# The second mixture ahead of the loop, as straight-line code

## The chip, the cores and the metric

One core of a Trainium2 chip runs the kernel. The metric is device time in microseconds, the median of three runs.

## The reference

Three layers follow each other on 4 batches of 576 tokens and 512 columns. The first two (a landmark attention and a gated feed-forward layer) end ahead of the change. The third, the mixture, is this:

```python
skip_score = x @ w_skip
do_compute = skip_score > 0
out = x.copy()
xc = x[do_compute]
logits = xc @ w_gate
e_idx = np.argmax(logits, axis=1)
...                                   # gate_w: softmax weight of the chosen expert
for e in range(E):                    # E = 8
    mask = e_idx == e
    if not mask.any():
        continue
    h = np.maximum(xc[mask] @ w1[e], 0.0)
    y[mask] = gate_w[mask, None] * (h @ w2[e])
out[do_compute] = xc + y
```

A token has one expert at most, w1 of an expert is 512 x 1024, w2 is 1024 x 512.

## The kernel before

The rows of x are handled in eight units of 288 tokens, two per batch. Each unit ends with a `finish` that writes x to `out` and the weight of each token for each expert to a table `m_d`, and sums these weights per batch and expert into `Ms`. The mixture works on pairs (expert e, batch b): a pair takes all 576 rows of a batch through one expert, and multiplies the result by the column of `m_d`, which is zero for tokens of other experts. Pairs whose sum in `Ms` is zero are left out, by a list made on the chip.

`list_pairs` (line 985) makes such a list: it flags the pairs with a sum over zero (`fl`), counts the flags ahead of each with a product by a triangular matrix, and by further small products puts the experts, the batches and the number of listed pairs into one row of integers, `lst`. It is called twice: in `early`, before the last unit, for the first pair, and in `others`, beside the first mixture, for the rest ("rest", without that first pair). `pair_at` (line 1025) reads entry i of a list into registers of SP, which alone uses them, as addresses of DMAs. `number` (line 1022) reads the length into registers of all engines, for the loop.

`mixture` (line 1101) does one pair, in straight order: for eight blocks f of 128 hidden columns it splits a block of w2 into a high and a low part (ScalarE, then GpSimd or VectorE), makes two accumulators `ph` (288 tokens each, 12 matmuls each: high by high, high by low, low by high, over four row blocks), and takes them out through ScalarE (the relu, high part) and VectorE (the remainder, low part). At f = 5 `load_rows` (line 1071) issues on SP the loads of the column of `m_d` (`mc`) and of the five blocks of `out` (`old`). After f = 7 it asks `nxt` for the next pair and issues that pair's loads on SP: x (`load_x`), w1 (`load_w1`), which are split at once, and w2 (`load_w2`), which stay raw until the next pair's blocks f. Then come the w2 products: five output blocks `py` (16 and four times 24 matmuls), each followed by a VectorE operation `old = py * mc + old` and a write of `old` to `out`. With `ahead` False a mixture loads its own w2 first; only the first mixture does.

The first mixture is straight-line code (lines 1350 to 1352). Behind it stands the loop over the list "rest" (lines 1354 to 1356), whose body is one mixture:

```python
npairs = number(rest[0])
with tc.For_i(0, npairs) as i:
    e, b = pair_at(rest[0], i)
    drain(mixture(e, b, lambda: pair_at(rest[0], i + 1), True))
```

All DMAs are issued by SP. Within a stretch of straight code, and within the loop's body, the compiler orders each engine's queue by its own plan, so a queue can differ from the order of the code. The accumulators `acc` are four banks, `pb` two (`bank`). `Paced` (line 36) books an estimate for every call of an engine into `busy`; in the last unit `slot` uses these sums to decide where side work goes.

Of the kernel before, what the change touches and what calls it, by code (L numbers as in the profile page):

```python
# [6 lines left out]
F32 = mybir.dt.float32  # L7
F32R = mybir.dt.float32r
I32 = mybir.dt.int32
ALU = mybir.AluOpType  # L10
# [20 lines left out]
LP = 40  # L31
# [31 lines left out]
def attention_moe_kernel(  # L63
# [4 lines left out]
    V, A, G, PE = (  # L68
        Paced(e, busy, n)
        for e, n in (  # L70
            (nc.vector, "V"), (nc.scalar, "A"), (nc.gpsimd, "G"), (nc.tensor, "P")
        )
    )
# [3 lines left out]
    def pool(stack, name, bufs=1, **kw):  # L77
        return stack.enter_context(tc.tile_pool(name=name, bufs=bufs, **kw))
# [31 lines left out]
    rt = pool(ph1, "rt")  # L110
# [7 lines left out]
    start, start1 = ExitStack(), ExitStack()  # L118
# [23 lines left out]
    def bank(name):  # L142
        return pb.tile([128, 512], F32, name=name, tag="b")
# [12 lines left out]
    ones = const.tile([128, 32], F32, name="ones")  # L156
# [828 lines left out]
    def list_pairs(name, but=None):  # L985

        pq = bank("pq")
        PE.matmul(
            pq[0:32, 0:1], Ms.rearrange("p b e -> p (b e)"), ones[:, 0:1],
            start=True, stop=True,  # L990
        )
        fl = rt.tile([32, 1], F32, name="fl")
        if but is None:
            V.tensor_scalar(fl, pq[0:32, 0:1], 0.0, None, ALU.is_gt)
        else:
            V.scalar_tensor_tensor(
                fl, pq[0:32, 0:1], 0.0, but, ALU.is_gt, ALU.subtract
            )
        pq = bank("pq")
        PE.matmul(pq[0:32, 0:1], tri, fl, start=True, stop=True)  # L1000
        ps = rt.tile([32, 1], F32, name="slot")
        V.tensor_copy(ps, pq[0:32, 0:1])
        oh = const.tile([32, LP], F32, name=f"oh{name}")
        V.tensor_scalar(oh, pos, ps, fl, ALU.is_equal, ALU.mult)
        pl = bank("pl")
        PE.matmul(pl[0:1, 0:LP], pair[:, 1:2], oh, start=True, stop=True)
        PE.matmul(pl[0:1, LP : 2 * LP], pair[:, 2:3], oh, start=True, stop=True)
        PE.matmul(
            pl[0:1, 2 * LP : 2 * LP + 1], fl, ones[0:32, 0:1], start=True, stop=True
        )  # L1010
        lst = const.tile([1, 2 * LP + 1], I32, name=name)
        V.tensor_copy(lst, pl[0:1, 0 : 2 * LP + 1])
        return lst, oh[:, 0:1]

    SPE = mybir.EngineType.SP

    def ld(lst, idx, mx):
        return nc.values_load(
            lst[0:1, bass.ds(idx, 1)], engines=(SPE,), min_val=0, max_val=mx
        )  # L1020

    def number(lst):
        return nc.values_load(lst[0:1, 2 * LP : 2 * LP + 1], min_val=0, max_val=B * E)

    def pair_at(lst, i):
        return ld(lst, i, E - 1), ld(lst, i + LP, B - 1)
# [29 lines left out]
    def w2raw(f):  # L1056

        return w2r_t[f // 2][:, f % 2]
# [7 lines left out]
    def load_x(b, c, eng):  # L1066
        r = late.tile([128, S], F32, name="x2r", tag="ld", bufs=4)
        SP.dma_start(r, xT_d[:, c, bass.ds(b * S, S)])
        rsplit(eng, xs[0][:, c], xs[1][:, c], r)

    def load_rows(e, b):

        mc = late.tile([128, 5], F32, name="mc")
        mrow = m_d[bass.ds(b * S, S), bass.ds(e, 1)]
        with nc.allow_non_contiguous_dma(reason="one column"):
            SP.dma_start(
                mc[:, 0:4], mrow[0:512].rearrange("(t p) o -> p (t o)", p=128)
            )
            SP.dma_start(mc[0:64, 4:5], mrow[512:576])
        orow = out[bass.ds(b * S, S), :]  # L1080
        olds = []
        for t in range(5):
            m = 128 if t < 4 else 64
            old = late.tile([128, DM], F32, name=f"old{t}")
            SP.dma_start(old[0:m], orow[128 * t : 128 * t + m, :])
            olds.append(old)
        return mc, orow, olds

    def early(res):

        lst, res["mark"] = list_pairs("lst")
        e, b = res["pair"] = pair_at(lst, 0)
        for c in range(KC):
            load_x(b, c, V if c % 2 else G)
        yield
        for i in range(2):
            for f in range(4 * i, 4 * i + 4):
                load_w1(e, f, V if f % 2 else G)
            yield

    def mixture(e, b, nxt, ahead):

        hs = []
        for f in range(FC2):
            if ahead:
                r = w2raw(f)
            else:
                r = late.tile([128, S], F32, name="w2r", tag="ld", bufs=4)[:, 0:DM]
                load_w2(e, f, r)
            rsplit(V if f % 2 else G, *w2s(f), r)  # L1110
            wh, wl = (t.rearrange("p (c f) -> p c f", c=KC) for t in w1s(f))

            hh, hx, hl = (
                hroom[f][:, s] for s in (slice(0, S), slice(512, 640), slice(640, None))
            )
            for t in range(2):
                ts = slice(NH * t, NH * t + NH)
                ps = accbank("ph")[:, 0:NH]
                for c in range(KC):
                    xh, xl = xs[0][:, c, ts], xs[1][:, c, ts]  # L1120
                    PE.matmul(ps, wh[:, c], xh, start=(c == 0), stop=False)
                    PE.matmul(ps, wh[:, c], xl, start=False, stop=False)
                    PE.matmul(ps, wl[:, c], xh, start=False, stop=(c == KC - 1))
                A.activation(hh[:, ts], ps, AF.Relu)
                n = (NH, 512 - NH)[t]
                V.scalar_tensor_tensor(
                    hl[:, NH * t : NH * t + n], ps[:, 0:n], 0.0,
                    hh[:, NH * t : NH * t + n].bitcast(F32), ALU.max, ALU.subtract,
                )
            V.scalar_tensor_tensor(  # L1130
                hx[:, 64:128], ps[:, n:NH], 0.0, hx[:, 0:64].bitcast(F32),
                ALU.max, ALU.subtract,
            )
            hs.append((hh, hx, hl))
            if f == FC2 - 3:
                mc, orow, olds = load_rows(e, b)
            yield
        en, bn = nxt()
        if not w2r_t:
            w2r_t.extend(wo_tile(F32) for _ in range(FC2 // 2))  # L1140
        for c in range(KC):
            load_x(bn, c, V)
        for f in range(FC2):
            load_w1(en, f, V if f % 2 else G)
        for f in range(FC2):
            load_w2(en, f, w2raw(f))

        ps = accbank("py")
        for f in range(FC2):
            for i, w in enumerate(w2s(f)):  # L1150
                PE.matmul(
                    ps, hs[f][1], w,
                    start=(f + i == 0), stop=(f + i == FC2),
                )
        old = olds[4][0:64]
        for p in (ps[0:64], ps[64:128]):
            V.scalar_tensor_tensor(old, p, mc[0:64, 4:5], old, ALU.mult, ALU.add)
        SP.dma_start(orow[512:S, :], old)
        yield
        for t in range(4):  # L1160
            ts = slice(128 * t, 128 * t + 128)
            old = olds[t]
            ps = accbank("py")
            for f in range(FC2):
                (hh, _, hl), (wh, wl) = hs[f], w2s(f)
                PE.matmul(ps, hh[:, ts], wh, start=(f == 0), stop=False)
                PE.matmul(ps, hh[:, ts], wl, start=False, stop=False)
                PE.matmul(ps, hl[:, ts], wh, start=False, stop=(f == FC2 - 1))
            V.scalar_tensor_tensor(
                old, ps, mc[:, t : t + 1], old, ALU.mult, ALU.add  # L1170
            )
            SP.dma_start(orow[ts, :], old)
            yield
# [14 lines left out]
    def drain(g):  # L1188
        for _ in g:
            pass  # L1190
        if g in side:
            side.remove(g)
# [103 lines left out]
    for u in range(1, 2 * B):  # L1296
        b, half = u // 2, u % 2
# [25 lines left out]
        if u == 2 * B - 2:  # L1323
# [5 lines left out]
            first = {}  # L1329
# [3 lines left out]
    rest = []  # L1333

    def others():
        yield from fin[0]
        rest.append(list_pairs("rest", first["mark"])[0])
        yield

    oth = others()  # L1340
# [2 lines left out]
    for g in side[:]:  # L1343
        drain(g)

    def after_first():
        drain(oth)
        return pair_at(rest[0], 0)

    for _ in mixture(*first["pair"], after_first, False):  # L1350
        next(oth, None)
        next(oth, None)
    npairs = number(rest[0])
    with tc.For_i(0, npairs) as i:  # L1354
        e, b = pair_at(rest[0], i)
        drain(mixture(e, b, lambda: pair_at(rest[0], i + 1), True))
    ph1.close()
    ctx.close()

# [32 lines left out]
```

## Time and profile before

| | us |
|---|---|
| runs: 726.9, 723.27, 725.94; median | 725.94 |
| the profiled execution | 730.47 |
| its span, first to last instruction | 728.7 |
| TensorE busy | 667.1 (92%) |
| VectorE busy | 459.2 (63%) |
| ScalarE busy | 295.1 (41%) |
| GpSimd busy | 145.1 (20%) |
| mean granted clock of TensorE | 0.952 of full speed |

Times in the rows are microseconds from the start of the span, unless they are means in ns. PE is TensorE's matmul, PEld its weight load, DVE VectorE, ACT ScalarE, POOL GpSimd, SP SyncE; a q behind a name is the engine's instruction queue. L12 is a line of the kernel; as all engine calls pass through the helper `call`, they have its line, L58, and are told apart by their tiles: `ph` are the w1 products of the mixtures, `py` their w2 products. Ends of matmuls are modelled. In the profiled execution the first mixture's `ph` begin at 557.9 us, and the two trips of the loop begin with `ph` at 613.57 and 669.83 us.

### The profile page before, as it was taken

The page shows a single profiled execution, that of the slowest core. Times are in us where ns is not written, and L with a number is a line of the kernel's source. Part 1 is how long each engine was busy: PE and PEld are TensorE (multiplying, and loading weights), DVE is VectorE, ACT ScalarE, POOL GpSimd, SP SyncE. Part 2 cuts the span into 40 slices and gives each one's busy share as a digit, 9 for nine tenths or more (in the row PEclk, how much of TensorE's full clock was granted, in tenths as well). Part 3 has the DMA queues.
Part 4 walks back from the last instruction along what each step waited for, and adds up shares of the span by engine and source line. Part 5 has one row for each costly group of instructions (what it writes and reads, how often), then busy time and mean ns, then how long its engine had stood idle before and what let it go on. Part 6 is the DMA issues. An engine that isn't in the chain of part 4 may idle for free. (4 is left out here: it accounts for less than half of the span.)

```text
span 728.7 us, 13382 instructions
## 1 busy us (share of the span) xinstructions
PE 667.1 (92%) x4961; PEld 573.5 (79%) x4961; DVE 459.2 (63%) x1016; ACT 295.1 (41%) x641; POOL 145.1 (20%) x162
## 2 busy tenths in 40 slices
PE   5468799789999899999999999999999999997997
PEld 5257367678877599977898897899889988986985
DVE  5984888978887577886467966261553463352451
ACT  0773887753314431433341344240443243241340
POOL 4000024313200140220040130040362023021120
PEclk8765799899999999999999999999999999998999
DMA  8686464573125842226732107230541375462344
GB/s 284 216 248 227 143 217 152 176 180 100 46 86 117 196 128 75 93 67 149 187 84 66 64 20 157 69 75 1 166 139 62 101 218 173 130 201 95 128 140 156
DMA packets 79435, 97.12 MB, mean 133 GB/s; under 512 B 16016, under 2 KB 58000, under 8 KB 79376
## 3 DMA queue, kind: packets, MB, share of 16 engines
q1 hardware_dynamic: 79376, 96.33, 44.9%
q8 instruction: 37, 0.61, 0.4%
q14 instruction: 22, 0.18, 0.1%
HBM read 76.97 MB, written 19.34 MB: 132 GB/s over the span
## 5 line engine op out<-in xcount | busy, mean ns | idle before, releaser
L58 PE MATMUL o<-h_t,wo 128*128 128x288 f32 x1152 | 169.6, 303 | 9.2 <-ACT wo L58 3.8
L58 PEld LDWEIGHTS o<-h_t,wo 128*128 128x128 f32 x1152 | 157.9, 191 | 19.2 <-issue 6.7
L58 POOL TENSOR_TENSOR h_t<-h,h_t 128x288 fp32r<-128x288 f32 x96 | 82.2, 860 | 399.9 <-ACT h_t L58 363.8
L58 PE MATMUL pg<-ap_t,P 128*128 128x288 f32 x576 | 104.1, 306 | 3.6 <-DVE h L58 1.8
L58 PE MATMUL pv<-ap_t,P 128*128 128x288 f32 x576 | 98.8, 301 | 2.7 <-DVE h L58 2.4
L58 PEld LDWEIGHTS pg<-ap_t,P 128*128 128x128 f32 x576 | 83.2, 189 | 17.6 <-issue 10.3
L58 PEld LDWEIGHTS pv<-ap_t,P 128*128 128x128 f32 x576 | 82.8, 189 | 8.8 <-DVE h L58 4.1
L58 PE MATMUL ph<-xsh,P 128*128 128x288 f32 x384 | 80.5, 303 | 4.5 <-PEq L1354 4.5
L58 PEld LDWEIGHTS ph<-xsh,P 128*128 128x128 f32 x384 | 64.0, 194 | 5.4 <-issue 5.4
L58 DVE SCALAR_TENSOR_TENSOR h<-h,pg 128x288 f32<-128x288 f32 x96 | 42.5, 447 | 26.3 <-ACT h L58 25.2
L58 PE MATMUL ph<-xsl,P 128*128 128x288 f32 x192 | 57.9, 302 | 0.0
L58 ACT ACTIVATE h<-pg 128x288 f32<-128x288 f32 x96 | 38.9, 410 | 42.4 <-PE pg L58 39.1
L58 ACT CAST h_t<-h 128x288 fp32r<-128x288 f32 x96 | 40.8, 430 | 32.6 <-DVE h L58 32.0
L58 PE MATMUL py<-wo,h_t 128*128 128x512 f32 x210 | 51.6, 395 | 0.3 <-DVE h_t L58 0.3
L58 PEld LDWEIGHTS py<-wo,h_t 128*128 128x128 f32 x210 | 39.3, 188 | 10.2 <-issue 0.8
L58 DVE TENSOR_TENSOR h<-h,pv 128x288 f32<-128x288 f32 x96 | 42.4, 446 | 5.9 <-PE pv L58 3.0
L58 DVE STREAM_TRANSPOSE T<-kq 64x576 f32<-64x576 f32 (+1 forms) x40 | 35.6, 889 | 9.0 <-DMA kq<-in_q_dram 4.6
L58 DVE TENSOR_TENSOR P<-P,P 128x512 fp32r<-128x512 f32 x48 | 31.7, 685 | 12.5 <-ACT P L58 12.1
L58 ACT CAST P<-P 128x512 fp32r<-128x512 f32 x48 | 26.3, 588 | 31.8 <-PE P L58 31.6
L58 PEld LDWEIGHTS ph<-xsl,P 128*128 128x128 f32 x192 | 37.4, 195 | 0.1
L58 POOL TENSOR_TENSOR P<-w1r,P 128x512 fp32r<-128x512 f32 x16 | 21.4, 1341 | 66.3 <-ACT P L58 66.3
L58 DVE SCALAR_TENSOR_TENSOR old<-py,mc,old 128x512 f32<-128x512 f32 (+1 forms) x18 | 13.5, 749 | 31.4 <-PE py L58 31.2
(230 smaller groups left out, 967.2 us busy)
## 6 DMA issues: line engine op xcount, KB each, us to landing
wl<-wg_d SPq DMA_DIRECT2D x36, 256.0 KB, 4.7
wr<-wv_d SPq DMA_DIRECT2D x32, 256.0 KB, 4.8
w1r<-in_moe_w_dram SPq DMA_DIRECT2D x32, 256.0 KB, 3.2
wr<-in_moe_w_gate_dram SPq DMA_DIRECT2D x6, 1024.0 KB, 6.6
wr<-in_moe_w_val_dram SPq DMA_DIRECT2D x6, 1024.0 KB, 6.1
wo<-in_moe_w_dram SPq DMA_DIRECT2D x24, 256.0 KB, 5.3
kq<-in_k_dram SPq DMA_DIRECT2D x8, 576.0 KB, 4.3
kq<-in_q_dram SPq DMA_DIRECT2D x8, 576.0 KB, 4.0
```

Source lines behind the costliest of these rows:

```text
L58: return f(*args, **kw)
```

## The change

The second pair gets a `mixture` of its own between the first mixture and the loop, as straight-line code, which runs whether or not there is a second pair. The loop runs over the pairs from the third on, so its trip count is the length of the list less one, and at least zero, and its indices are one higher. Where the list is empty, `pair_at` reads expert 0 and batch 0; so that nothing is then added to `out`, `list_pairs` also makes `any_`, a column of 128 values that is 1 where the list has an entry and else 0 (one more matmul, into a bank of `pb`, and one more VectorE operation), and the second mixture multiplies its `mc` by it, in two VectorE operations behind `load_rows` at f = 5. The copy of the list to integers becomes two operations, as the length is clamped to 1 and lowered by 1 on the way. The call in `early` makes `any_` too and doesn't use it.

```diff
--- before.py
+++ after.py
@@ -1009,8 +1009,20 @@
             pl[0:1, 2 * LP : 2 * LP + 1], fl, ones[0:32, 0:1], start=True, stop=True
         )
         lst = const.tile([1, 2 * LP + 1], I32, name=name)
-        V.tensor_copy(lst, pl[0:1, 0 : 2 * LP + 1])
-        return lst, oh[:, 0:1]
+        V.tensor_copy(lst[:, 0 : 2 * LP], pl[0:1, 0 : 2 * LP])
+
+        V.tensor_scalar(
+            lst[:, 2 * LP :], pl[0:1, 2 * LP : 2 * LP + 1], 1.0, 1.0,
+            ALU.max, ALU.subtract,
+        )
+        pn = bank("pn")
+        PE.matmul(
+            pn[:, 0:1], fl.to_broadcast([32, 128]), ones[0:32, 0:1],
+            start=True, stop=True,
+        )
+        any_ = rt.tile([128, 1], F32, name="any")
+        V.tensor_scalar(any_, pn[:, 0:1], 1.0, None, ALU.min)
+        return lst, oh[:, 0:1], any_
 
     SPE = mybir.EngineType.SP
 
@@ -1088,7 +1100,7 @@
 
     def early(res):
 
-        lst, res["mark"] = list_pairs("lst")
+        lst, res["mark"], _ = list_pairs("lst")
         e, b = res["pair"] = pair_at(lst, 0)
         for c in range(KC):
             load_x(b, c, V if c % 2 else G)
@@ -1098,7 +1110,7 @@
                 load_w1(e, f, V if f % 2 else G)
             yield
 
-    def mixture(e, b, nxt, ahead):
+    def mixture(e, b, nxt, ahead, any_=None):
 
         hs = []
         for f in range(FC2):
@@ -1134,6 +1146,11 @@
             hs.append((hh, hx, hl))
             if f == FC2 - 3:
                 mc, orow, olds = load_rows(e, b)
+                if any_ is not None:
+                    V.tensor_scalar(mc[:, 0:4], mc[:, 0:4], any_, None, ALU.mult)
+                    V.tensor_scalar(
+                        mc[0:64, 4:5], mc[0:64, 4:5], any_[0:64], None, ALU.mult
+                    )
             yield
         en, bn = nxt()
         if not w2r_t:
@@ -1334,7 +1351,7 @@
 
     def others():
         yield from fin[0]
-        rest.append(list_pairs("rest", first["mark"])[0])
+        rest.extend(list_pairs("rest", first["mark"])[0::2])
         yield
 
     oth = others()
@@ -1343,17 +1360,21 @@
     for g in side[:]:
         drain(g)
 
+    second = []
+
     def after_first():
         drain(oth)
-        return pair_at(rest[0], 0)
+        second.append(pair_at(rest[0], 0))
+        return second[0]
 
     for _ in mixture(*first["pair"], after_first, False):
         next(oth, None)
         next(oth, None)
+    drain(mixture(*second[0], lambda: pair_at(rest[0], 1), True, rest[1]))
     npairs = number(rest[0])
     with tc.For_i(0, npairs) as i:
-        e, b = pair_at(rest[0], i)
-        drain(mixture(e, b, lambda: pair_at(rest[0], i + 1), True))
+        e, b = pair_at(rest[0], i + 1)
+        drain(mixture(e, b, lambda: pair_at(rest[0], i + 2), True))
     ph1.close()
     ctx.close()
 
```

## Rows read from the trace of the kernel before

**Rows 1.** The page's engine table: busy us (share of the span) and instructions.

```profile
PE 667.1 (92%) x4961; PEld 573.5 (79%) x4961; DVE 459.2 (63%) x1016; ACT 295.1 (41%) x641; POOL 145.1 (20%) x162
```

**Rows 2.** The page's DMA issues: KB each, median us to landing.

```profile
w1r<-in_moe_w_dram SPq DMA_DIRECT2D x32, 256.0 KB, 3.2
```

**Rows 3.** Stages: length; busy us of PE, PEld, DVE, ACT, POOL; PEclk, DMA, GB/s.

```profile
555.00:613.55 58.55, 58.20 (x359) 51.52 (x359) 27.55 (x59) 22.02 (x45) 13.32 (x10) 1.00 0.53 167
613.55:665.40 51.85, 51.80 (x305) 46.36 (x303) 22.25 (x43) 15.78 (x32) 8.17 (x6) 1.00 0.49 150
665.40:669.80 4.40, 0.00 (x0) 0.00 (x0) 0.74 (x1) 0.03 (x1) 0.00 (x0) 0.87 0.16 60
669.80:675.00 5.20, 5.17 (x21) 5.20 (x22) 3.79 (x4) 4.00 (x8) 3.81 (x3) 0.50 0.26 65
676.00:724.30 48.30, 48.20 (x279) 42.79 (x277) 18.66 (x38) 13.72 (x28) 6.31 (x5) 1.00 0.45 141
```

**Rows 4.** Timeline between the trips: start, us, engine, instruction [idle before, releaser].

```profile
665.39 0.75 DVE L58 SCALAR_TENSOR_TENSOR old<-py,mc,old 128x512 f32<-128x512 f32 x1 [4.84 <-PE py L58]
666.16 0.33 SPq L1172 DMA_DIRECT2D out_dram<-old  x1
...
669.83 0.58 PE L58 MATMUL ph<-xsh,P 128*128 128x288 f32 x1 [4.48 <-PEq L1354]
...
670.45 0.69 PE L58 MATMUL ph<-xsh,P 128*128 128x288 f32 x2
```

**Rows 5.** List of line L1354, the loop: ns min/median/max, first and last start.

```profile
L1354 SPq EVENT_SEMAPHORE  x27: 17/28/28, 666.9 to 727.3; - x27
...
L1354 PEldq EVENT_SEMAPHORE  x11: 51/51/51, 668.7 to 727.6; - x11
...
L1354 PEldq COMPARE_BRANCH  x4: 80/217/245, 610.1 to 727.7; - x4
```

**Rows 6.** Waits of SP's queue, 613 to 729: us in total, times, longest.

```profile
SPq L1048 <- DVE xsl L58: 31.7, 4, 18.1
...
SPq L1354 <- DMA out_dram<-old: 2.3, 2, 1.3
```

**Rows 7.** Table of DMA issues: KB each, median us from issue to landing.

```profile
out_dram<-old SPq DMA_DIRECT2D x12, 256.0 KB, 2.0
...
mc<-m_d SPq DMA_DIRECT2D x3, 2.0 KB, 1.9
```

**Rows 8.** Stages for the tile ph alone, PE, PEld, DVE, ACT; PEclk.

```profile
613.55:639.00 25.45, 25.43 (x192) 25.41 (x191) 7.29 (x22) 6.17 (x15) 1.00 0.37 105
669.80:698.05 28.25, 28.22 (x192) 28.04 (x192) 7.31 (x22) 6.16 (x15) 0.90 0.28 84
```

**Rows 9.** Timeline of TensorE, from the first mixture into trip 1.

```profile
610.07 3.66 PE L58 MATMUL py<-wo,h_t 128*128 128x512 f32 x15
613.57 0.29 PE L58 MATMUL ph<-xsh,P 128*128 128x288 f32 x1
...
613.83 0.43 PE L58 MATMUL ph<-xsh,P 128*128 128x288 f32 x2
```

**Rows 10.** List of the tile rest: TensorE's queue loads the length.

```profile
L1023 PEldq TENSOR_LOAD <-rest x1: 488/488/488, 609.4 to 609.4; - x1
```

**Rows 11.** Timeline of TensorE in the first mixture's w2 products.

```profile
590.63 0.70 PE L58 MATMUL py<-wo,h_t 128*128 128x512 f32 x2 [0.35 <-DVE h_t L58]
```

**Rows 12.** Timeline of the second call of list_pairs, in the first mixture.

```profile
573.08 0.22 PE L58 MATMUL pq<-ones,Ms 128*32 128x1 f32 x2
...
573.95 0.15 DVE L58 COPY slot<-pq 32x1 f32<-32x1 f32 x1 [0.46 <-PE pq L58]
```

**Rows 13.** Timeline of SP's queue in trip 1.

```profile
618.14 0.56 SPq L1079 DMA_DIRECT2D mc<-m_d  x1
...
640.27 6.58 SPq L1048 DMA_DIRECT2D w1r<-in_moe_w_dram  x6
647.07 0.55 SPq L1158 DMA_DIRECT2D out_dram<-old  x1
```

## The prediction

> **What bounds the kernel now.** I read the page from the top and then only the last 170 us, where the change lies. The engine table [rows 1] has TensorE busy in 92% of the span: its idle time is what to look for. The DMA table [rows 2] tells how often the loop runs. `early` and each call of `mixture` load eight blocks of w1; 32 loads are four times eight: `early`, the first mixture, and two trips of the loop. So with these inputs the list "rest" holds two pairs, and the loop's end is passed twice, once as a back edge (trip 1 to trip 2) and once as the exit.
>
> The table of stages [rows 3] is the main view. In mixture 1, with what runs just ahead of it (555 to 613.55 us), TensorE is busy 58.20 of 58.55 us; in trip 1, 51.80 of 51.85; in trip 2 from 676 us on, 48.20 of 48.30. Between the trips, 665.40 to 669.80, stands no matmul at all, and behind that a stretch in which TensorE is busy but its granted clock is 0.50, the lower of its two levels (1.2 GHz). In the mixtures no other engine sets the pace (in trip 1 VectorE has 22.25 us of 51.85, ScalarE 15.78).
>
> The timeline of the gap [rows 4] shows what it consists of. TensorE's idle time of 4.48 us ends at 669.83, so it began at 665.35; VectorE takes 0.75 us for the last output block, SP issues its write at 666.16. The list of line L1354, the loop [rows 5], has semaphore events on every queue, SP's first at 666.9 and TensorE's first at 668.7; the waits of SP's queue put its wait in that line down to the write of `old` [rows 6], and such a write lands 2.0 us after its issue [rows 7]: 666.16 + 2.0 is 668.2, just ahead of those events. So the trip ends when its last write has landed and all engines have met. The page's chain of waits begins at that meeting and says nothing of the time before; I don't use it.
>
> **The change part by part.**
>
> *Removed: one back edge.* The gap is 4.48 us by TensorE's own row [rows 4]. The clock behind it: the 192 w1 products of trip 2 have TensorE for 28.22 us, those of trip 1 for 25.43 [rows 8], so the lower clock costs 2.79 us. Together 7.27 us. The exit stays: the last events of L1354 are at 727.6 [rows 5], and the new kernel leaves its loop once, as the old.
>
> A rule of the Trainium skill can be weighed here, as it would cut the gain. The row has a granted clock of 0.50 for 669.8 to 675.0 [rows 3]. The Trainium skill, "TensorE: Matmul & The Clock Gate", in the trace caveats of its Part 1, warns that clock events in traces have been seen to be unreliable and should be cross-checked; if this record were wrong, the second term would fall away and the gain would be 4.48 us. The cross-check is in the durations: a pair of the same matmuls takes 0.69 us behind the gap [rows 4] and 0.43 at the start of trip 1 [rows 9]. Record and durations agree, so the term stays.
>
> *Put in its place: two seams*, mixture 1 to mixture 2 and mixture 2 to the loop. For the second the trace has the very row: TensorE goes from the last w2 products of mixture 1 (the group from 610.07) to the first w1 product of trip 1 at 613.57 with no idle time [rows 9]. At that seam each engine loads the trip count and branches; TensorE's queue did the load at 609.4 in 0.49 us [rows 10], 4 us ahead of its matmuls, under queued products. That cover gone, it would cost 0.49 and a branch of 0.22 [rows 5], 0.7 us. The first seam has the same data to wait for, without count and branch. I take 0 for both, between 0 and 0.7.
>
> *The second mixture as straight code* has the same matmuls, DMAs and vector work as a trip. The nearest row for straight code is mixture 1, whose w2 products meet one wait of 0.35 us for VectorE [rows 11], as the finish of the last unit and `load_w2` share the engines there. Mixture 2 has neither, its w2 being loaded ahead. I take 0; the bounds are a loss of 0.35 and, if the new order of mixture 1 takes the wait away, a gain of 0.35.
>
> *New instructions in `list_pairs`,* which is called twice (in the last unit and in mixture 1): each time one matmul of 128 columns of weights and 1 of data. The nearest row is the first product of the same function, 0.22 us in TensorE's stream [rows 12]. It has a quarter of the columns, so I keep 0 (hidden in an issue gap) and twice that row, 0.44, as bounds, and take 0.22: 0.44 us for both calls, 0 to 0.88. On VectorE come two more operations per call of about 0.15 us, as the small copy [rows 12]; VectorE is idle for over half of both stages [rows 3], so they cost 0; uncovered they would be 0.6 us in all.
>
> *The pacing* (`Paced`) books these calls before it places the side work of the last unit: 121 more for VectorE (two calls at 61, less one element of the copy), 12 for TensorE, by its own formula. That can move a step of side work by one slot. I take 0, with 0.35 to either side, the one wait that such neighbours left [rows 11].
>
> *The product of the m column with `any`*: two VectorE operations of about 0.15 us, in f = 5 of mixture 2. They bring a new wait, for the load of `mc`. VectorE runs in order: behind them stand the remainders of f = 5 to 7, and behind those the accumulators that TensorE writes. In trip 1 the loads of `mc` are issued by 618.14 [rows 13] and land 1.9 us later [rows 7], at 620.0, while f = 5 comes at 613.57 + 5 x 3.18 = 629.5 (25.43 us for eight). Ten us of lead: 0. SP's queue moves nothing else: the two list reads per pair, the loads and the writes are those of a trip.
>
> Sum: -4.48 - 2.79 + 0.44 = -6.83 us. The profiled execution took 730.47 us with a span of 728.7; it would come to 723.6. The median of the runs is 725.94, 4.5 us lower; the gap is in the program whichever run it is, so the same difference goes off the median: **719.1 us**. Bounds of the gain: 7.27 - 0.88 - 0.7 - 0.35 - 0.35 - 0.6 = 4.4 at least and 7.27 + 0.35 + 0.35 = 8.0 at most, so 717.9 to 721.5.
>
> **The rivals.**
>
> A, part comes back at a seam. Mixtures 1 and 2 are now one stretch of code whose queues are ordered together, and an order that puts a split of a later block ahead of an eviction would hold TensorE. For it: a queue is not in the code's order even now (on SP the write of L1158 stands behind six of the eight w1 loads of L1048 [rows 13]; in the code it is behind all eight and the w2 loads too). Against it: mixture 1, ordered together with all that precedes it, has only the 0.35 us. Price: half the old gap with half its clock term, 3.6 us: 722.7.
>
> B, the straight copy doesn't escape the meeting: a seam with the loop waits for writes to land, as its end does, and the gap only moves. 725.9 and the 0.44 of the new products: 726.4. For it: SP waited twice in L1354 for a write [rows 6]. Against it: the start of trip 1 at 613.57 without idle time [rows 9]; the second wait is then the exit's. That there is no second trip to save is excluded by the 32 loads [rows 2].
>
> C, slower: the m column comes late. If its load stands on SP behind the w1 loads of the next pair, which wait for buffers, 18.1 us at the longest [rows 6], and run from 640.27 to 647 [rows 13], it lands near 649, and VectorE stands from 629.5. The four accumulators at 1.59 us each (25.43 over 16) let TensorE go on for 6.4 us at most; it then stops for 649 - 629.5 - 6.4 = 13.1 us and pays the clock again (2.8): 719.1 + 15.9 = 735. It decides from a landing later than 635.9, some 16 us after that of trip 1. Against it: in the code this load precedes those w1 loads, and it needs only the buffer that mixture 1 frees at its end.
>
> **How the numbers follow.** Forecast 0.80, A 0.10, B 0.06, C 0.04. About 0.5% (3.6 us, also the distance between the runs of before) is what a measurement of this kernel can tell from no change. Faster than 722.3 are the forecast and a third of A: 0.83; the same, the rest of A and B: 0.13; slower, C: 0.04. The range holds the forecast's bounds, the spread of the runs (2.7 below the median, 1.0 above) in part, and half of A: 716.0 to 722.7.
>
> **What would show it.** Right: TensorE without an idle row of a microsecond from the first w1 product of mixture 1 to the last w2 product of the trip; granted clock 1.00 over all of it; three w1 stages of about 25.4 us of TensorE each; the loop's drains only once, at the end; two small products on `mc`, near the start or the middle of mixture 2, without a wait. Wrong: an idle row of TensorE at either seam, with its releaser (A, B); a wait of VectorE for a load of `mc` (C); or these stages as forecast and the time elsewhere, ahead of 555 us, where only the pacing step reaches.

## The result

The changed kernel takes 721.34 us (median of 20 runs, 718.01 to 729.05), the kernel before 727.47 in 20 runs beside it (723.27 to 732.96). The ratio is 0.9913, with a 95% interval of 0.9892 to 0.9934: 6.3 us less (4.8 to 7.9); it leaves out the one run of 729.05 us, which counts as a slow one. The profiled execution took 723.82 us with a span of 722.1, against 730.47 and 728.7.

The page's engine table, which answers to [rows 1], differs little: TensorE is busy in 92% of the span as before, and for 2.6 us less, about what the third pair's stage loses below with the lower clock.

```profile
PE 664.5 (92%) x4965; PEld 573.5 (79%) x4965; DVE 458.4 (63%) x1022; ACT 295.9 (41%) x641; POOL 144.8 (20%) x162
```

The table of stages, cut within 0.03 us of where a mixture's first w1 product starts, tells where the time went. First the changed kernel (columns as in [rows 3]): mixture 1, mixture 2, the one trip, the tail from the last VectorE operation on.

```profile
557.28:613.64 56.36, 55.79 (x341) 49.08 (x340) 28.15 (x63) 21.60 (x44) 12.68 (x10) 1.00 0.56 171
613.64:665.33 51.69, 51.69 (x306) 46.55 (x305) 20.94 (x42) 17.05 (x34) 10.21 (x8) 1.00 0.48 154
665.33:717.23 51.90, 51.87 (x305) 46.38 (x303) 22.02 (x42) 15.77 (x32) 8.23 (x6) 1.00 0.49 150
717.23:722.10 4.87, 0.00 (x0) 0.00 (x0) 0.75 (x1) 0.00 (x0) 0.00 (x0) 0.77 0.16 57
```

The kernel before with the same cuts: mixture 1, trip 1, the gap, trip 2, the tail.

```profile
557.89:613.57 55.68, 55.33 (x338) 48.63 (x337) 26.00 (x58) 19.84 (x41) 11.29 (x9) 1.00 0.56 176
613.57:665.35 51.78, 51.78 (x305) 46.36 (x303) 22.23 (x42) 15.78 (x32) 8.17 (x6) 1.00 0.49 150
665.35:669.83 4.48, 0.00 (x0) 0.03 (x1) 0.75 (x1) 0.06 (x1) 0.00 (x0) 0.87 0.16 59
669.83:724.24 54.41, 54.37 (x304) 48.96 (x304) 23.36 (x41) 17.99 (x36) 11.12 (x8) 0.95 0.44 137
724.24:728.70 4.46, 0.00 (x0) 0.00 (x0) 0.75 (x1) 0.00 (x0) 0.00 (x0) 0.77 0.17 62
```

Line by line, after less before: -0.61 ahead of the mixtures, +0.68 in mixture 1, -0.09 in the second pair, -4.48 for the gap, -2.51 in the third pair, +0.41 in the tail: -6.6, the difference of the spans. The gap is gone, and so is the lower clock of the third pair. What is measured from the first w1 product to the start of the last VectorE operation, 166.35 us before and 159.95 after, I call the mixture stage below; it is free of what happens before the mixtures, where runs of one kernel differ (two profiles of one kernel below, e3 and e11, begin their mixtures at 557.29 and 554.05).

Both seams in the timeline of TensorE, which answer to [rows 9] and [rows 4], have no idle time in brackets. The only idle row of TensorE from 557 us to the end is the old wait in mixture 1 of [rows 11], now 0.57 instead of 0.35.

```profile
590.58 0.71 PE L58 MATMUL py<-wo,h_t 128*128 128x512 f32 x2 [0.57 <-DVE h_t L58]
...
612.67 1.10 PE L58 MATMUL py<-wo,h_t 128*128 128x512 f32 x4
613.61 0.30 PE L58 MATMUL ph<-xsh,P 128*128 128x288 f32 x1
...
661.81 3.68 PE L58 MATMUL py<-wo,h_t 128*128 128x512 f32 x15
665.33 0.29 PE L58 MATMUL ph<-xsh,P 128*128 128x288 f32 x1
```

The w1 products of the second and third pair, which answer to [rows 8], are now alike, at the higher clock:

```profile
613.75:639.20 25.45, 25.45 (x192) 25.27 (x191) 7.29 (x22) 6.17 (x15) 1.00 0.34 109
665.45:690.95 25.50, 25.50 (x192) 25.27 (x191) 7.29 (x22) 6.17 (x15) 1.00 0.35 104
```

The new product of `list_pairs` in mixture 1 stands in the stream from 574.74 to 575.05, 0.31 us. The products on `mc` are found at 619.49 in the timeline of VectorE, behind a wait:

```profile
574.74 0.38 PE L58 MATMUL pn<-ones,fl 32*128 32x1 f32 x2
575.05 0.40 PE L58 MATMUL ph<-xsl,P 128*128 128x288 f32 x1
...
619.49 0.34 DVE L58 TENSOR_SCALAR mc<-mc,any 128x4 f32<-128x4 f32 x2 [1.53 <-DMA mc<-m_d]
```

The page counts 39 packets of q8, the instruction fetch, against 37 before.

### The profile page after: what moved, and what is told of

Its sections match the earlier page's. It is cut to its first block, busy times and chain, and to the rows that moved or that the text cites. A ratio compares the mean times of both kernels' runs of the same rounds, so it can differ in the third digit from the quotient of the medians.

```text
span 722.1 us, 13338 instructions
## 1 busy us (share of the span) xinstructions
PE 664.5 (92%) x4965; PEld 573.5 (79%) x4965; DVE 458.4 (63%) x1022; ACT 295.9 (41%) x641; POOL 144.8 (20%) x162
## 4 chain that ended last, share of the span: by engine, by line
PE 60%; DVE 6%; DMA 2%; ACT 2%; issue 1%; SPq 0%; ACTq 0%; DVEq 0%
PE o L58 15%; PE py L58 10%; PE ph L58 10%; PE pv L58 7%; PE pg L58 7%; PE P L58 3%; PE sq L58 2%; DVE T L58 1%; DMA x2r<-xT_d 1%; PE nr L58 1%; PE x2t L58 1%; DVE ln L58 1%; DVE h L58 1%; PE rb L58 1%; DMA w1r<-in_moe_w_dram 1%
## 5 line engine op out<-in xcount | busy, mean ns | idle before, releaser
L58 PE MATMUL o<-h_t,wo 128*128 128x288 f32 x1152 | 172.0, 305 | 9.0 <-ACT wo L58 3.8
L58 PEld LDWEIGHTS o<-h_t,wo 128*128 128x128 f32 x1152 | 160.3, 194 | 19.1 <-issue 6.7
L58 PE MATMUL ph<-xsh,P 128*128 128x288 f32 x384 | 78.1, 296 | 0.0
L58 PEld LDWEIGHTS ph<-xsh,P 128*128 128x128 f32 x384 | 62.0, 188 | 0.6 <-issue 0.5
L58 DVE SCALAR_TENSOR_TENSOR h<-h,pg 128x288 f32<-128x288 f32 x96 | 42.5, 447 | 25.4 <-ACT h L58 24.2
L58 DVE SCALAR_TENSOR_TENSOR h_t<-ph,h_t 128x288 fp32r<-128x288 f32 (+2 forms) x45 | 14.7, 353 | 29.5 <-ACT h_t L58 29.5
```

Source lines behind the costliest of these rows:

```text
L58: return f(*args, **kw)
```

## The experiments

The theory: the change saves one back edge, that is, the time in which all engines meet behind the landing of the last write, and the lower clock behind it; that code stands outside the loop is worth nothing by itself. The rivals: the gain is that of straight code, or of not coming back to a long body; the price isn't the meeting; the clock falls for another reason than the idle time; the new operations cost more than they show. In all that follows ratios are to the kernel before, on the same chip; stages, tails and idle rows are from one profile of each kernel.

### Both mixtures in one trip

The kernel before, with two mixtures in the loop's body.

```diff
-    with tc.For_i(0, npairs) as i:
+    with tc.For_i(0, npairs, 2) as i:
         e, b = pair_at(rest[0], i)
-        drain(mixture(e, b, lambda: pair_at(rest[0], i + 1), True))
...                                                # after_one: nx = [pair_at(rest[0], i + 1)]
+        drain(mixture(e, b, after_one, True))
+        drain(mixture(*nx[0], lambda: pair_at(rest[0], i + 2), True))
```

> The kernel before (its lists, no clamp, no product on mc) with two mixtures in each trip of the loop, step two; it is only right for a list of even length, as here. Both mixtures are inside the loop, and the back edge isn't taken with two pairs. If only the back edge counts, this gains what the change gains and keeps the 0.44 us of the new products: -7.3 us, ratio 0.990 (0.987 to 0.993), seam in the trip without idle time. If the gain came from code being outside the loop, it stays at 1.000.

Measured: 719.61 us, ratio 0.9902 (0.9866 to 0.9938); mixture stage 159.24 us, 7.11 less than before. The seam inside the trip:

```profile
659.03 3.66 PE L58 MATMUL py<-wo,h_t 128*128 128x512 f32 x15
662.52 0.30 PE L58 MATMUL ph<-xsh,P 128*128 128x288 f32 x1
```

Both pairs are in the loop and the gain is there. It is the back edge that counts, not where the code stands.

### The third pair as straight code, with and without a loop behind it

```diff
...
-    drain(mixture(*second[0], lambda: pair_at(rest[0], 1), True, rest[1]))
...                                   # after_second: third = [pair_at(rest[0], 1)]
+    drain(mixture(*second[0], after_second, True, rest[1]))
+    drain(mixture(*third[0], lambda: pair_at(rest[0], 2), True))
     npairs = number(rest[0])           # clamped to 2 and lowered by 2
     with tc.For_i(0, npairs) as i:
-        e, b = pair_at(rest[0], i + 1)
+        e, b = pair_at(rest[0], i + 2)
...
```

> The changed kernel with the third pair's mixture as straight code too; the loop behind it has no trip with these inputs (the third mixture has no product on mc, so it is only right if there is a third pair, as here). If a gain comes once per back edge that is saved, there is none left: within 1 us of the changed kernel, ratio 0.989 to 0.993; at most the meeting at the loop's exit is left out, some tenths of a us, as the last write has to land in any case. If each mixture that leaves the loop gains by being straight code, another 6 us: ratio 0.983.

Measured: 722.99 us, ratio 0.9940 (0.9903 to 0.9976), so it is slower than forecast by some 3 us. The mixture stage is 159.30 us, against 159.95 for the changed kernel: no further gain per straight mixture, as the theory has it. The loss is in the tail, 8.31 us, and the list of the loop's line L1382 shows what stands in it: on TensorE's queue a branch of 3.53 us, from 716.7 on, where the last matmul has just ended.

```profile
557.30:716.59 159.29, 159.25 (x948) 142.01 (x946) 73.38 (x146) 54.98 (x109) 31.85 (x23) 1.00 0.51 159
716.59:724.90 8.31, 0.00 (x0) 0.00 (x0) 0.75 (x1) 0.00 (x0) 0.00 (x0) 0.71 0.11 38
...
L1382 PEldq COMPARE_BRANCH  x1: 3530/3530/3530, 716.7 to 716.7; - x1
...
q8 instruction: 41, 0.67, 0.4%
```

To see whether passing over the loop is the cause, the same kernel once more, and one without the loop (and without `number`) beside it on one chip.

> The kernel of e3 (second and third mixture as straight code) without the loop behind them, so it is only right for three pairs in all, as here. In e3 the time from the last matmul to the end was 8.28 us against 4.90 in the changed kernel, and TensorE's queue had a branch of 3.53 us there. If that is the price of passing over a loop that has no trip, it goes away: 4 to 5 us from the last matmul to the end, 3 to 4 us less than e3, ratio 0.986 to 0.990. If e3 lost its time through its third mixture as such, this kernel stays where e3 was, 0.994.

> The kernel of e3 again, beside e10 on the same chip: two straight mixtures and a loop without a trip. 8.3 us from the last matmul to the end, ratio 0.992 to 0.996, 3 to 4 us over e10.

Measured: e10 without the loop 720.66 us, ratio 0.9879 (0.9830 to 0.9929); e11 with it 725.17 us, 0.9963 (0.9931 to 0.9995), a little above what was expected. Their tails, e10 first:

```profile
719.23:723.10 3.87, 0.00 (x0) 0.00 (x0) 0.75 (x1) 0.00 (x0) 0.00 (x0) 1.00 0.18 68
713.67:722.00 8.33, 0.00 (x0) 0.00 (x0) 0.75 (x1) 0.00 (x0) 0.00 (x0) 0.66 0.13 40
```

The mixture stages are the same, 159.89 and 159.62, and the tail differs by 4.5 us, as the medians do. In e11 the branch takes 3.63 us. So a loop that is passed over without a trip costs 4.5 us here, while the tails behind one trip (4.87) or two (4.46) are only 0.6 to 1.0 us longer than that without a loop. The Trainium skill, "Runtime: NRT & Kernel Launch", under "Instruction fetch mechanics", says that a taken branch to a target outside the pages at hand has to wait for a fetch by DMA; the trace fits that for this branch: 3.53 us, 41 packets of q8 against 39 in e10 and in the changed kernel, and in e11 two packets of instructions while the branch lasts (713.6 to 717.4). Whose instructions they carry, the rows don't say.

```profile
q8 instruction: 1, 0.02, 2.2%
q14 instruction: 1, 0.01, 0.5%
```

The back edge of the kernel before shows no such branch on TensorE's queue: its longest is 0.245 us [rows 5]. It has no packet of instructions either, nor has any time from 650 to 715 us, where this one queue is all that moves:

```profile
q1 hardware_dynamic: 9182, 9.65, 47.1%
```

So the rival that the price lies in fetching the code of a long body again is out for the back edge.

### An empty loop at the seam

A loop of one trip between mixtures 1 and 2 of the changed kernel.

```diff
+    with tc.For_i(0, 1) as j:
+        V.memset(rt.tile([32, 1], F32, name="nil"), 0.0)
     drain(mixture(*second[0], lambda: pair_at(rest[0], 1), True, rest[1]))
```

> The changed kernel with one thing more: between mixture 1 and mixture 2 stands a loop of one trip whose body is one clearing of 32 values on VectorE. If the price of the old back edge is the meeting of all engines behind the landing of the last write, with the clock that falls behind it, this empty trip brings it back at the first seam: TensorE idle for 4.5 us (4 to 6), granted clock 0.50 for some 5.6 us behind it, +7 us over the changed kernel, so a ratio to the kernel before of 1.000 (0.997 to 1.004). If the price lay in coming back to a long loop body (its code, its tiles), an empty trip has next to none of it: idle under 1 us, ratio 0.991 to 0.993.

Measured: 720.96 us, ratio 0.9917 (0.9881 to 0.9952). This tells nothing on the seam: the compiler put the loop, which depends on nothing, at the start of the program.

```profile
L58 DVE MEMSET nil<- x1: 59/59/59, 1.2 to 1.2; 32x1 f32 x1
```

So the loop was tied to its place: the last quarter of x for mixture 2 is split with a bias z, zero times a column of mixture 1's last output block, and z is made in the loop. The same kernel without the loop is its control (e6).

```diff
...
+            with tc.For_i(0, 1) as j:                          # e8 only
                 V.tensor_scalar(z, olds[3][:, 0:1], 0.0, None, ALU.mult)
             load_x(bn, KC - 1, V, z)                           # A.activation(hi, r, AF.Identity, bias=z)
...
```

> As the run before, but the split of the last quarter of x waits only for the last VectorE operation of mixture 1, not for the write and a read: idle time at the seam some 2 us (0.75 + 0.2 + 0.7 + 0.7, less the matmuls that need only the other quarters). It shows whether an idle time of less than half the old gap brings the lower clock too: if so 0.50 behind it and +4.8 us over the changed kernel; if not, clock 1.00 and +2 us.

> The empty trip once more, now tied to its place: the kernel of e6 (the split of the last quarter of x waits for a value made from the last output block), with that one small VectorE operation as the body of a loop of one trip. Without the loop this seam had 1.36 us of idle time and no fall of the clock. If the loop's end, with all engines meeting behind the landing of the last write, is the price of the old back edge, TensorE now idles 4.5 to 6.5 us, the granted clock is 0.50 behind it, and the time is 7 to 9 us over the changed kernel: ratio 1.000 to 1.004. If the loop's end is cheap when the body is short, the seam stays near 1.4 us and the ratio near 0.993.

Measured: e6 722.40 us in one run, mixture stage 161.58; e8 726.06 us, ratio 0.9952 (0.9922 to 0.9981), mixture stage 163.69. The seams: in e6, `z`, TensorE's idle row and the stage behind it; in e8, the same, the writes on SP's queue, and the loop's events on TensorE's queue.

```profile
613.36 0.14 DVE L58 TENSOR_SCALAR z<-old 128x1 f32<-128x1 f32 x1
614.36 0.67 PE L58 MATMUL ph<-xsh,P 128*128 128x288 f32 x3 [1.36 <-ACT xsh L58]
614.40:620.00 5.60, 5.60 (x42) 5.60 (x43) 2.82 (x9) 1.53 (x4) 0.00 (x0) 1.00 0.71 194
```

```profile
606.70 10.05 SPq L1192 DMA_DIRECT2D out_dram<-old  x4
615.81 0.14 DVE L58 TENSOR_SCALAR z<-old 128x1 f32<-128x1 f32 x1
616.45 0.40 PE L58 MATMUL ph<-xsl,P 128*128 128x288 f32 x1 [2.42 <-DVE z L58]
616.45:620.00 3.55, 3.55 (x26) 3.55 (x27) 1.72 (x5) 1.43 (x3) 0.00 (x0) 1.00 0.45 95
L1196 PEldq EVENT_SEMAPHORE  x6: 51/51/1894, 613.7 to 616.1; - x6
```

In e8 the loop's end brings 1.06 us of idle time more than its control has, not the 4.5 to 6.5 in all that I expected, and the clock stays. (The other 1.07 us between their mixture stages is the wait of [rows 11], 1.32 us in e8 and 0.25 in e6.) `z` is made no later than in the control: 2.88 us behind the seam's first product, 2.92 in e6 (behind 612.93 and 610.44). But TensorE stands at the loop from 614.03 on, 1.10 us behind that product, where in e6 it goes on for 2.56 us with products that don't need `z`; and it starts 0.50 us behind the end of `z`, at 616.45. SP's queue tells why it is no second back edge: the fourth write is issued at the end of that group (606.70 and 10.05, 616.75), behind the loop's last event at 616.1, so this loop's end did not wait for it to land; and it is an exit, not a way back. Both expectations of e8 fail in part. What it shows is a meeting without a write: 0.50 us behind the last engine to come, and 1.06 us of idle time here in all, as TensorE came early and could do nothing meanwhile. It leaves the rest of the gap to the write and to what a back edge has more than an exit, which the next run takes apart.

### The last write left out

```diff
-            SP.dma_start(orow[ts, :], old)
+            if t < 3 or not ahead:
+                SP.dma_start(orow[ts, :], old)
```

> The kernel before, with the write of the fourth output block (of t = 3) left out in both trips of the loop; its 128 rows of out then lack the last part of the sum. It takes the landing of the last write out of the back edge: the write before it is issued 5.6 us earlier and has landed. If the gap of 4.48 us is that landing (some 2.3 us) and the meeting (the rest), TensorE idles 2.0 to 2.5 us between the trips, and whether the clock falls behind that shows in the rows (after 1.36 us it didn't, after 4.48 it did): 2.2 us less than the kernel before at the back edge and as much at the exit, ratio 0.994, or 2.8 us less again, 0.990. If the meeting alone takes the time, the gap stays above 4 us and the ratio at 0.997 to 1.000.

Measured: 723.93 us, ratio 0.9914 (0.9878 to 0.9951); mixture stage 163.21, 3.14 less than before; tail 2.10 instead of 4.46. The back edge, and the stage behind the restart:

```profile
665.37 0.75 DVE L58 SCALAR_TENSOR_TENSOR old<-py,mc,old 128x512 f32<-128x512 f32 x1 [4.84 <-PE py L58]
667.70 0.37 PE L58 MATMUL ph<-xsh,P 128*128 128x288 f32 x1 [2.37 <-PEq L1355]
...
668.50:673.00 4.50, 4.50 (x24) 4.50 (x23) 4.20 (x4) 3.60 (x9) 4.50 (x4) 0.62 0.36 80
```

The gap is 2.37 us, within the 2.0 to 2.5 of the first forecast, and the ratio lies between the two that were given for it; so of the 4.48 the landing of the write had 2.11. Of the 2.37, 0.75 are the last VectorE operation; it ends at 666.12, and TensorE starts 1.58 us later: that is the back edge itself, with its drains and meetings, against the 0.50 behind `z` at the exit of e8. The clock fell behind this shorter gap too, from some 0.9 us after the restart; the w1 products, from the first of them to the first w2 product, took 27.08 us (667.70 to 694.78), 1.59 over the 25.49 of trip 1 in the kernel before, at the higher clock.

### A stall without a loop

The changed kernel, with `z` made from a value that is read back from the last output block behind its write. No loop stands at this seam.

```diff
...
+            SP.dma_start(zr, orow[384:512, 0:1])
+            V.tensor_scalar(z, zr, 0.0, None, ALU.mult)
+            load_x(bn, KC - 1, V, z)
```

> The changed kernel with a stall of another cause at the first seam, without a loop and without a meeting: the split of the last quarter of x for mixture 2 is made to wait for a value that is read back from the last output block of mixture 1 after its write (multiplied by zero, so the numbers stay). TensorE then idles at the seam for about 0.75 (last VectorE operation) + 0.3 + 2.0 (write) + 0.4 + 2.0 (read) + 0.2 + 0.7 + 0.7 (split) = 7 us, less the few matmuls that don't need this quarter. If the clock falls because TensorE is idle, whatever the cause, the rows show 0.50 behind it and the price is the idle time and 2.8 us more: +8 to +10 us over the changed kernel, ratio 1.003. If the lower clock belongs to the drain and meeting of the loop's end, the clock stays at 1.00: +5 to +7 us, ratio 0.999.

Measured: 728.90 us, ratio 1.0003 (0.9964 to 1.0043), mixture stage 168.44, 8.5 more than the changed kernel. The idle row at the seam, and the stage behind it:

```profile
625.97 1.33 PE L58 MATMUL ph<-xsh,P 128*128 128x288 f32 x4 [5.48 <-ACT xsh L58]
...
625.97:632.00 6.03, 6.03 (x26) 6.03 (x27) 2.77 (x8) 1.64 (x4) 0.00 (x0) 0.53 0.99 302
```

5.48 us of idle time and the lower clock for nearly all of the next 6 us, without a loop, a drain or a meeting: the fall of the clock needs none of these, only TensorE standing still. The ratio can't tell the two forecasts apart (0.999 and 1.003 both lie in its interval); the rows do. How long TensorE stands still does not decide alone. 1.36 us (e6) and 2.42 (e8) left the clock at 1.00, and so did the 3.87 us without a matmul at the end of e10; behind 2.37 (e9) and 4.48 (before) it fell. What else decides stays open.

### The new operations without the straight mixture

The kernel before with the new `list_pairs` and, in each trip, the products on `mc`.

```diff
                 mc, orow, olds = load_rows(e, b)
+                if any_ is not None:
+                    V.tensor_scalar(mc[:, 0:4], mc[:, 0:4], any_, None, ALU.mult)
...
-        drain(mixture(e, b, lambda: pair_at(rest[0], i + 1), True))
+        drain(mixture(e, b, lambda: pair_at(rest[0], i + 1), True, rest[1]))
```

> The kernel before with what the change adds and without the second straight mixture: the new product and clamp in both calls of list_pairs, and the two products on mc in each trip of the loop (both pairs stay in the loop). Forecast of the parts: 0.44 us on TensorE (0 to 0.88), nothing on VectorE: ratio 1.000 to 1.002, back edge as before (idle 4.5 us, then the lower clock). If the new waits cost more than forecast (the products on mc hold VectorE, or the small products hold TensorE), +2 us or more, 1.003 or higher, and the back edge would be worth that much more than the change gained.

Measured: 728.54 us, ratio 1.0021 (0.9984 to 1.0057), mixture stage 167.17, 0.82 more than before. TensorE's idle rows in it, and VectorE's wait in trip 1:

```profile
587.68 0.71 PE L58 MATMUL py<-wo,h_t 128*128 128x512 f32 x2 [0.96 <-DVE h_t L58]
616.50 0.23 DVE L58 TENSOR_SCALAR mc<-mc,any 128x4 f32<-128x4 f32 x1 [3.41 <-DMA mc<-m_d]
617.74 0.40 PE L58 MATMUL ph<-xsh,P 128*128 128x288 f32 x1 [0.49 <-DVE P L58]
...
667.90 0.58 PE L58 MATMUL ph<-xsh,P 128*128 128x288 f32 x1 [4.55 <-PEq L1371]
```

The ratio is compatible with the forecast and with the rival of 2 us. By the rows, mixture 1 is 1.05 us longer than before (0.61 of it the longer wait at 587.68), trip 1 is 0.85 longer (0.49 of it TensorE's wait behind the product on `mc`), and trip 2 is 1.15 shorter: its w1 products take 26.83 us (667.90 to 694.73), so the lower clock cost 1.34 us here instead of 2.76. The two losses, 1.90 us, are of the rival's size; the total hides them behind the smaller price of the clock. In the loop, where VectorE takes the splits of w2 at the start of a trip, the early product on `mc` does hold TensorE; in the changed kernel, whose second pair takes 51.69 us, it does not.

### The column of mc later

The changed kernel with the two loads of `mc` issued behind the five of `old`.

```diff
...
             olds.append(old)
+        with nc.allow_non_contiguous_dma(reason="one column"):
+            SP.dma_start(
+                mc[:, 0:4], mrow[0:512].rearrange("(t p) o -> p (t o)", p=128)
+            )
+            SP.dma_start(mc[0:64, 4:5], mrow[512:576])
```

> The changed kernel with the loads of mc issued behind the five loads of old in load_rows, so that in mixture 2 they land some 2.7 us later (five issues of 0.53 us). In the changed kernel the product on mc stood early in VectorE's queue and waited 1.5 us for that load, without a wait of TensorE. If the four accumulators cover such a wait, VectorE now waits some 4 us, or the plan puts the product later, and TensorE still goes through the seam without idle time. If the cover is thinner than 4 us, TensorE shows an idle row of 1 us or more with a VectorE or ScalarE operation as its releaser.

Measured, in one run: 720.26 us, mixture stage 159.22, no idle row of TensorE in it. VectorE waits 3.33 us for the load, behind the split of w2 and not ahead of it:

```profile
622.49 0.23 DVE L58 TENSOR_SCALAR mc<-mc,any 128x4 f32<-128x4 f32 x1 [3.33 <-DMA mc<-m_d]
```

So the accumulators cover a wait of this length there; about the same length cost 0.49 us in e4, where the splits of w2 stood behind it.

## Why the prediction was right

It was right in sign, mechanism and size: 719.1 us was forecast, in a range from 716.0 to 722.7, and 721.34 measured. Of the 2.2 us between them, 1.5 are the kernel before itself, which came to 727.47 in 20 runs and not to the 725.94 of the three. As a difference, 6.83 us were forecast; the profile has 6.6, the ratio 6.3 (4.8 to 7.9).

That the hit is so near is in part luck: the interval of the runs, 4.8 to 7.9, covers the gain with every value that the clock's term takes below (5.4 to 6.8), so it says little on the size of that term.

*The gap, 4.48 us*: gone, as forecast, and e2 shows that the back edge was its cause and not the place of the code. Its parts, only argued in the prediction from the times of the write, are now measured: 0.75 the last VectorE operation, 2.11 the landing of the write (e9), the rest, about 1.6, the back edge itself.

*The clock, 2.79 us*: 2.51 by the third pair's stages. That it belongs to the idle time and not to the loop is shown by e5, which has it without one. But it is no constant: 1.34 us behind the same kind of back edge in e4, 1.59 behind the shorter gap of e9, 2.76 in the kernel before. In rows of half a microsecond, the one in which the clock falls and the one in which it rises, for before, e9 and e4:

```profile
668.50:669.00 0.50, 0.00 (x0) 0.00 (x0) 0.00 (x0) 0.00 (x0) 0.00 (x0) 0.62 0.00 0
675.00:675.50 0.50, 0.50 (x4) 0.50 (x4) 0.50 (x1) 0.10 (x1) 0.50 (x2) 0.55 1.05 393
...
668.50:669.00 0.50, 0.50 (x4) 0.50 (x3) 0.20 (x1) 0.50 (x2) 0.50 (x1) 0.58 0.00 0
671.50:672.00 0.50, 0.50 (x4) 0.50 (x4) 0.50 (x2) 0.50 (x2) 0.50 (x1) 0.51 0.92 119
...
667.00:667.50 0.50, 0.00 (x0) 0.00 (x0) 0.00 (x0) 0.00 (x0) 0.00 (x0) 0.81 0.00 0
670.50:671.00 0.50, 0.50 (x5) 0.50 (x5) 0.00 (x0) 0.00 (x0) 0.50 (x1) 0.78 0.38 3
```

TensorE worked at the lower clock until 675.4 before, to 672.0 in e9 and to 670.7 in e4: 5.6, 3.4 and 2.8 us of work. Half of each, 2.8, 1.7 and 1.4, is about what the w1 products lost. Why the clock came back sooner in two of the three stays open. The forecast took the value of one execution and gave it no bounds; with 1.3 the gain would have been 5.4. This step was mis-sized in its certainty, not in this profile.

*The seams, 0*: right, at both (613.61 and 665.33 in the timeline above). *The second mixture as straight code, 0*: right, 51.69 us against 51.78.

*The new products, 0.22 us each*: the one that can be read takes 0.31 us of the stream, inside the bounds of 0 to 0.44. Mixture 1 is 0.68 us longer in all: 0.31 for this, 0.22 for the longer wait at 590.58, the rest not placed. Its w1 products take 27.20 us, as before (27.19) and not the 25.4 that the prediction named for all three, because other products stand among them; the sum doesn't use that figure. The wait differs from profile to profile (none in e3 and e7, 0.24 in e11, 1.32 in e8), so it is no fixed price of the change. Against e2, which has none of the new operations, the mixture stage of the changed kernel is 0.71 us longer, and that of e7, which has them all, as long (159.22). The first call, and the pacing step, lie ahead of the mixtures, where the profiles of one kernel differ by 3 us; they cannot be read.

*The products on mc, 0*: the price was right and the working was not. I put them at f = 5, 629.5 us, ten us behind the landing. The compiler's queue has them at 619.49, and they waited 1.53 us for the load. What made the wait free was the cover of the accumulators, which the text used in rival C alone: e7 has no idle row of TensorE behind 3.33 us of wait, and e4 shows that the cover can fail (0.49 us). That a queue differs from the order of the code stood in the prediction for SP [rows 13] and should have been held against this step as well.

*The tail, 0*: it is 0.41 us longer. The tails of the kernels here that have at least one trip and all writes lie between 4.34 and 4.96 without a pattern that I can name, so I give it no cause.

*The rivals*: A and B fall with the seams, B also with e2; C's mechanism was there in small (1.53 us), and far from the 6.4 us of cover from which it was to decide.

## What to carry to other kernels

A back edge is priced in the trace where it stands: the idle row of the engine that bounds the kernel, and behind it the stage in which that engine runs slower than the same stage did before; both go when the trip goes, whether the body is unrolled inside the loop or put ahead of it. Let the stage answer, not the total: from the first w1 product on, the stages of the kernels here without a stall repeat within 0.7 us (159.22 to 159.95), while the runs are 5 us and more apart. And count the trips that are left: here an exit behind a trip cost at most 1.0 us, and a loop that was passed over 4.5.

## What the runs showed of the hardware

- A loop without a trip cost 4.5 us (tail 8.33 in e11 against 3.87 in e10), 3.63 of them a branch on TensorE's queue that no matmul covered. The changed kernel would meet such a branch with inputs of fewer pairs; that was not run.
- The landing of one write of 256 KB is 2.11 us of the 4.48 at the back edge. Leaving the write out took 2.4 us off the exit as well (2.10 in e9 against 4.46). A write that lands earlier should shorten both; that was not run.
- TensorE stood idle for 2.42 us in e8 and kept its clock, and for 2.37 in e9 and lost it: 0.62 on the mean from 668.5 to 673.0. The lower clock, once it came, cost 1.3 to 2.8 us, about half of the time that TensorE worked at it.
